# First block of a three-stage kernel: token sums spread over three chunks, seven-product sets from chunk 3 on, squares of chunk 0 on ScalarE

## The chip, the cores and the metric

One NeuronCore of a Trainium2 chip runs the whole program. The metric is the device time in microseconds, the median of several executions.

## The reference

Three stages follow one another. Retention attention (4 batches, 8 heads, 576 positions, 64 per head) gives x of 2304 tokens by 512. A first feed-forward block takes x through 2048 hidden units with a squared ReLU. A second one takes the result through four domains of 1024 hidden units each, weighted by normalised probabilities.

```python
scores = scale * np.matmul(q, k.transpose(0, 1, 3, 2))
attn_out = np.matmul(scores * Dmat[None, :, :, :], v)
x = attn_out.transpose(0, 2, 1, 3).reshape(B * S, H * D)
...
r = np.maximum(x @ w_in, 0.0)
x = (r * r) @ w_out
...
p = domain_probs / (domain_probs.sum(-1, keepdims=True) + 1e-09)
for e in range(4):
    out += p[:, e:e + 1] * (np.maximum(x @ w1[e], 0.0) @ w2[e])
```

The weights of the first block arrive as 64-bit floats.

## The kernel before, in words

Every matrix is split in two fp32r parts, high and low, and a product of two matrices is three products of parts (high by high, high by low, low by high). Tokens lie in five groups: groups 0 to 3 of 512 tokens and group 4 of 256. A chunk is 256 hidden units: chunks 0 to 7 are the first block, later ones the second. For a chunk `layer1` makes two halves (`f`) of 128 hidden units, twelve products each; `square` (line 598) takes ReLU, square, a high copy on ScalarE and a low part on GpSimd (`split`, line 132), with the square on ScalarE or VectorE by its argument `act`. `layer2_1` (line 875) makes four results of six products from them and writes or adds them to `yacc` (lines 888 to 891).

For chunks in `sevens` (line 66) the groups 0 and 1, and 2 and 3, go in pairs through `layer1_seven` (line 675), which makes a two by two block product with seven block products (42 instructions) instead of eight (48). It needs sums of weight blocks (S1 to S4, lines 156 to 173, made with the conversion of the chunk's weights) and sums of token blocks (T1 to T4). The token sums are made once for each pair by the generator `combine` (line 647): four sums on GpSimd, and four times a difference on VectorE (line 663), a high copy on ScalarE (line 668), a low part on VectorE (line 670) and two stores to DRAM (line 673), for each of two halves. As SBUF has no room for both pairs, `load_parts` (line 638) puts reloads from DRAM into the list `pulls`, and `pull` issues one at a time between the products; all of them are DMAs on SyncE's queue, as are the loads of raw weights (`load_piece`, line 80), which wait for a free one of three buffers.

The order of each engine is the order in which the program writes instructions. Background work is a list `work` of generators, and `tick(n)` (line 267) takes n steps from its front. A step is about one VectorE instruction. `from_f64` (line 101) converts one piece of a weight chunk in six steps: five VectorE instructions (lines 114, 116, 118, 120, 125), a magnitude and a high copy on ScalarE, an addition and a subtraction on GpSimd (lines 128 and 129). A chunk has eight pieces, four for each layer. `queue_weights` (line 287) appends the conversion of a chunk two ahead as its buffers come free. `mix` (line 622) weaves `combine` into it, one step of each in turn, the first pair into chunk 1's weights, the second into those of layer 1 of chunk 2. `pace[0]` (line 1182) is the number of steps behind each half of layer 1 and each result of layer 2: 4 in chunks 0 and 1, 2 in chunks 2 to 5. In a set two steps stand behind each block product, ahead of the additions that read it.

The jobs (line 1140) are the layer 1 parts in order; behind each come the layer 2 parts that `behind` names, or all but the latest. Before the first set, in chunk 2, its token sums must be back in SBUF: at job (1, (3,)) the program drains the conversion woven with the second pair's sums, and queues the eight reloads.

Of the kernel before, what the change touches and what calls it, by code (L numbers as in the profile page):

```python
# [26 lines left out]
NW1, NW2 = 8, 16  # L27
# [6 lines left out]
def tile_kernel(ctx, tc, qT, kT, kn, vn, v4d, mask, qdec, kdec, wd, w, probs, probs2, out, outT):  # L34
    nc = tc.nc
# [27 lines left out]
            return slot(t, 2 * g + k // 2)[:, k % 2, :]  # L63
        return t[2][:, GS[4] * k : GS[4] * k + GS[4]]

    sevens = range(2, NW1 - 2)

    def f32(ap):
        return ap.bitcast(F32)
# [195 lines left out]
    work = []  # L265
# [18 lines left out]

    held = {(split_w2, NW1), (split_w1, NW1 + 1)}

    def queue_weights(*place):
        free.update(place)
        while order and order[0] in free and order[0] not in held:
            f, c = order.pop(0)  # L290
            if c >= NW1 + NW2:
                work.extend(stores)
                stores.clear()
                fetch(f, c)
                continue
            splits[f, c] = f(c)
            work.append(splits[f, c])
            work.extend(stores)
            stores.clear()
            if c >= NW1:  # L300
                stores.append(keep(f, c))
# [233 lines left out]
    with tc.manual_schedule():  # L535
# [32 lines left out]
        pace = [2]  # L568
# [6 lines left out]
        def layer1(c, g, between=lambda: None):  # L575
            w1h, w1l = w1s[c]
            wk = lambda t, f, k: t[:, ((A11, A12), (A21, A22))[f][k // 2], k % 2, :]
            hi, lo = hidden(g)
            for f in range(FT):
                h = ps.tile([128, GT], F32, name="h", tag="ps")[:, : GS[g]]  # L580
                n = 0
                for k in range(KT):
                    for a, x in ((w1h, xh_), (w1h, xl_), (w1l, xh_)):
                        nc.tensor.matmul(h, wk(a, f, k), group(x, g, k), start=(n == 0), stop=(n == 3 * KT - 1))  # L584
                        n += 1
                if c < NW1:
                    r = tp.tile([128, GT], F32, name="r")[:, : GS[g]]
                    square(h, r, hi[:, f, :], lo[:, f, :], c in sevens or c == 1)
                else:
                    relu_split(h, hi[:, f, :], lo[:, f, :])  # L590
                tick(pace[0])
                pull()
                if f == 0:
                    extra = between()
            gh[c, g], gl[c, g] = hi, lo
            return extra

        def square(h, r, hi, lo, act=True, stay=False):
            nc.scalar.activation(out=r, in_=h, func=ACTF.Relu)
            if act:  # L600
                nc.scalar.activation(out=r, in_=r, func=ACTF.Square)
            else:
                nc.vector.tensor_tensor(out=r, in0=r, in1=r, op=ALU.mult)
            if stay:
                nc.scalar.copy(out=hi, in_=r)
                nc.vector.tensor_tensor(out=lo, in0=r, in1=f32(hi), op=ALU.subtract)
            else:
                split(r, hi, lo)
# [4 lines left out]
        def pull():  # L613
            if pulls:
                pulls.pop(0)()

        def saved(pair, i, y):
            if (pair, i, y) not in parted:
                parted[pair, i, y] = dram.tile([128, 2 * GT], F32, name=f"parted{pair}_{i}_{y}")
            return parted[pair, i, y].rearrange("p (k n) -> p k n", k=2)  # L620

        def mix(*todo):
            own = [splits[t] for t in todo[:-1]]

            def both():
                for g in own:
                    for _ in g:
                        yield
                        if next(todo[-1], 0) is None:
                            yield  # L630
                yield from todo[-1]

            m = both()
            j = min(j for j, x in enumerate(work) if any(x is g for g in own))
            work[:] = work[:j] + [m] + [x for x in work[j:] if not any(x is g for g in own)]
            splits.update({t: m for t in todo[:-1]})

        def load_parts(pair, what):

# [35 lines left out]
        def layer1_seven(c, ga, gb):  # L675

            w1h, w1l = w1s[c]
            pair = ga // 2
            s = 4 * pair
            own = lambda i: [slot(xh_, s + i), slot(xl_, s + i)]  # L680
            (ha, la), (hb, lb) = hidden(ga), hidden(gb)
            bank = lambda: ps.tile([128, GT], F32, name="h", tag="ps")
            v = nc.vector

            def product(o, i, x, first=True):
                n = 0
                for k in range(2):
                    for a, y in ((w1h, 0), (w1h, 1), (w1l, 0)):
                        nc.tensor.matmul(
                            o, a[:, i, k, :], x[y][:, k, :], start=(first and n == 0), stop=(n == 5),  # L690
                            skip_group_check=True,
                        )
                        n += 1
                tick(2)

            def add(o, x, y):
                v.tensor_tensor(out=o, in0=x, in1=y, op=ALU.add)

            if (c, pair) == (sevens[-1], 1):
                load_parts(0, [("b12", (slot(xh_, 2), slot(xl_, 2)))])  # L700
                load_parts(1, [("b12", (slot(xh_, 6), slot(xl_, 6)))])
            else:
                load_parts(1 - pair, [(i, bufs[i]) for i in (T2, T3, T1, T4)])
            u = [tp.tile([128, GT], F32, name="r") for _ in range(2)]
            u.append(cvp.tile([128, GT], F32, name="cv_tp"))
            b1 = bank()
            product(b1, A11, own(0))
            nc.scalar.copy(out=u[0], in_=b1)
            b6 = bank()
            product(b6, S2, bufs[T2])  # L710
            add(u[1], b6, u[0])
            b7 = bank()
            product(b7, S3, bufs[T3])
            add(u[2], b7, u[1])
            product(b1, A12, own(1), False)
            square(b1, b1, ha[:, 0, :], la[:, 0, :], stay=True)
            pull()
            b5 = bank()
            product(b5, S1, bufs[T1])
            add(u[2], b5, u[2])  # L720
            square(u[2], u[2], hb[:, 1, :], lb[:, 1, :])
            pull()
            product(b7, A22, bufs[T4], False)
            add(u[0], b7, u[1])
            square(u[0], u[0], ha[:, 1, :], la[:, 1, :])
            pull()
            product(b5, S4, own(3), False)
            add(u[1], b5, u[1])
            square(u[1], u[1], hb[:, 0, :], lb[:, 0, :])
            pull()  # L730
            gh[c, ga], gl[c, ga] = ha, la
            gh[c, gb], gl[c, gb] = hb, lb
# [142 lines left out]
        def layer2_1(c, g):  # L875
            w2h, w2l = w2s[c]
            hi, lo = gh.pop((c, g)), gl.pop((c, g))
            for m in range(KT):
                o = ps.tile([128, GT], F32, name="o", tag="ps")[:, : GS[g]]
                n = 0  # L880
                for f in range(FT):
                    for a, x in ((w2h, hi), (w2h, lo), (w2l, hi)):
                        nc.tensor.matmul(  # L883
                            o, a[:, f, 128 * m : 128 * m + 128], x[:, f, :], start=(n == 0), stop=(n == 3 * FT - 1)
                        )
                        n += 1
                y = yacc[g][:, m, :]
                if c == 0:
                    nc.scalar.copy(out=y, in_=o)  # L889
                else:  # L890
                    nc.vector.tensor_tensor(out=y, in0=o, in1=y, op=ALU.add)  # L891
                tick(pace[0])
                pull()
                if c == NW1 - 1 and g < 2:
                    magnitude(g, m, mags[g][m])
                if c == NW1 - 1 and g == NG - 1:
                    split(y, group(xh_, g, m), group(xl_, g, m))
# [263 lines left out]
        bufs["raw"] = [wp.tile([128, 2 * GT], F32, name=f"raw_{n}", tag=n) for n in ("r2hi", "r2lo")]  # L1161
        wide = lambda: [wp.tile([128, 2 * GT], F32R, name=n).rearrange("p (k n) -> p k n", k=2) for n in ("r2hi", "r2lo")]
        bufs["half"] = wide()
        combos = [combine(0), combine(1)]
        for i in range(2):
            for y, t in enumerate((xh_, xl_)):
                nc.sync.dma_start(out=saved(i, "b12", y), in_=f32(slot(t, 4 * i + 2)))
# [8 lines left out]
        for i, job in enumerate(jobs):  # L1176
# [2 lines left out]
            if c < NW1 + NW2:  # L1179
                drain(splits[split_w1, c])  # L1180

            pace[0] = 4 if c in (0, 1) else 3 if c in (p, q) else 4 if c == z else 3 if c >= NW1 and c not in scaled else 2
            if job == (1, (3,)):
                drain(splits[split_w1, 2])
                bufs.update({T2: (slot(xh_, 2), slot(xl_, 2)), T3: bufs["half"], T1: wide(), T4: (slot(xh_, 6), slot(xl_, 6))})
                load_parts(0, [(t, bufs[t]) for t in (T2, T3, T1, T4)])
            if c in sevens:
                while pulls:
                    pull()
# [37 lines left out]
            if g and gs == (4,):  # L1227
                rescale(g, s)
                if g == 3:
                    work.append(sb[0])  # L1230
            if job == (0, (0,)):
                mix((split_w1, 1), (split_w2, 1), combos[0])
            if job == (0, (4,)):
                mix((split_w1, 2), combos[1])
            pend += [(c, (g_,)) for g_ in gs] if c < NW1 else [job]
            todo = behind.get(job)
            if todo is None:
# [104 lines left out]
```

## Time and profile before

| | us |
|---|---|
| median of three runs | 1269.88 |
| lowest and highest of them | 1269.33, 1270.60 |
| the profiled execution, its own time | 1266.78 |
| its span, first to last instruction | 1265.0 |
| PE busy in the span | 1201.6 (95%) |
| VectorE (DVE) busy | 948.8 (75%) |
| GpSimd (POOL) busy | 704.5 (56%) |
| ScalarE (ACT) busy | 478.8 (38%) |

The profile's times start with the first instruction of one execution. PE is TensorE, PEld its loading of weights, SP the engine SyncE, whose queue issues the DMAs. An instruction's duration runs from its start to its end, with any time that it was held after its start in it. A wait is the idle time of an engine ahead of an instruction and is put down to what ended it. The attention stage ends and the first block starts at about 80 us; the second block starts at about 480 us.

### The profile page before, as it was taken

To read this page: it belongs to the slowest core of one execution; us is meant where nothing else is said; L and a number is where in the kernel's file an instruction comes from. 1 tells how busy PE (TensorE), PEld (TensorE's weight loads), DVE (VectorE), ACT (ScalarE), POOL (GpSimd) and SP (SyncE) were. 2 spreads that over 40 slices of the span, in tenths; PEclk is the share of its full clock that TensorE was granted. 3 is DMA by queue.
4 is the path that set the end of the run, shared out by engine and by line. 5 is a ranking of instruction groups with operands and counts; after the bars stand their busy time and mean duration, and the time that the engine had idled before them with its cause. 6 is when DMAs were issued, how large, how long until landed. Compare 5 with 4: busy or idle time off the path is not lost. (4 is left out here: it accounts for less than half of the span.)

```text
span 1265.0 us, 18570 instructions
## 1 busy us (share of the span) xinstructions
PE 1201.6 (95%) x6422; PEld 997.1 (79%) x6422; DVE 948.8 (75%) x1566; ACT 478.8 (38%) x1122; POOL 704.5 (56%) x713
## 2 busy tenths in 40 slices
PE   7999787998999999999999999999999999999997
PEld 6877575776887888788888888888787888888876
DVE  4789988968668658856786777776677778778768
ACT  4554555545444235453433323333322222222221
POOL 5748665544434334454445533555406777777775
PEclk9999898999999999999999999999999999999999
DMA  9942337547553100156525454454667664654651
GB/s 338 319 145 102 131 138 293 211 167 257 188 210 123 36 9 16 62 185 224 206 80 221 175 191 159 151 217 174 258 231 270 206 215 156 211 196 164 222 166 67
DMA packets 93538, 224.27 MB, mean 177 GB/s; under 512 B 11266, under 2 KB 19970, under 8 KB 93444
## 3 DMA queue, kind: packets, MB, share of 16 engines
q1 hardware_dynamic: 92932, 222.38, 49.7%
q8 instruction: 51, 0.84, 0.3%
q10 hardware_dynamic: 512, 0.70, 0.2%
q14 instruction: 43, 0.35, 0.1%
HBM read 149.88 MB, written 73.16 MB: 176 GB/s over the span
## 5 line engine op out<-in xcount | busy, mean ns | idle before, releaser
L923 DVE SCALAR_TENSOR_TENSOR oacc<-o,pr,oacc 128x512 f32<-128x512 f32 x150 | 110.0, 746 | 30.3 <-PE o L915 29.9
L883 PE MATMUL o<-glo,w2hi 128*128 128x512 f32 (+1 forms) x320 | 120.2, 376 | 12.4 <-POOL glo L134 12.4
L1058 DVE TENSOR_TENSOR sums<-sums,h 128x512 f32<-128x512 f32 x202 | 128.5, 678 | 1.9 <-PE h L1048 1.9
L915 PE MATMUL o<-w2hi,ghi 128*128 128x512 f32 x320 | 124.9, 390 | 0.5 <-ACT w2hi L133 0.4
L915 PE MATMUL o<-w2lo,ghi 128*128 128x512 f32 x320 | 124.7, 390 | 0.6 <-POOL w2lo L134 0.6
L915 PE MATMUL o<-w2hi,glo 128*128 128x512 f32 x320 | 124.7, 390 | 0.0
L134 POOL TENSOR_TENSOR glo<-r,ghi 128x512 fp32r<-128x512 f32 (+1 forms) x64 | 78.6, 1232 | 80.9 <-ACT ghi L133 68.8
L883 PE MATMUL o<-ghi,w2hi 128*128 128x512 f32 (+1 forms) x320 | 119.7, 374 | 1.3 <-ACT y L889 1.2
L883 PE MATMUL o<-ghi,w2lo 128*128 128x512 f32 (+1 forms) x320 | 119.3, 373 | 0.0
L891 DVE TENSOR_TENSOR y<-o,y 128x512 f32<-128x512 f32 (+1 forms) x140 | 87.0, 630 | 26.6 <-PE o L883 26.2
L584 PE MATMUL h<-xh,w1hi 128*128 128x256 f32 (+1 forms) x320 | 104.5, 326 | 2.5 <-ACT y L889 1.6
L134 POOL TENSOR_TENSOR w2lo<-wraw,w2hi 128x256 fp32r<-128x256 f32 x64 | 52.0, 837 | 98.1 <-ACT w2hi L133 98.1
L584 PE MATMUL h<-xl,w1hi 128*128 128x256 f32 (+1 forms) x320 | 104.1, 325 | 0.0
L584 PE MATMUL h<-xh,w1lo 128*128 128x256 f32 (+1 forms) x320 | 104.1, 325 | 0.0
L128 POOL TENSOR_TENSOR cv_m<-cv_m,cv_d 128x256 f32<-128x256 f32 x64 | 50.9, 795 | 86.3 <-DVE cv_d L125 74.9
L966 PE MATMUL h<-xh,w1hi 128*128 128x512 f32 x224 | 88.3, 394 | 3.6 <-ACT r L985 2.6
L753 PE MATMUL h<-xh,w1lo 128*128 128x512 f32 x224 | 88.0, 393 | 2.2 <-POOL w1lo L134 2.2
L753 PE MATMUL h<-xh,w1hi 128*128 128x512 f32 x224 | 88.1, 393 | 2.1 <-ACT r L766 1.1
L753 PE MATMUL h<-xl,w1hi 128*128 128x512 f32 x224 | 87.7, 392 | 0.0
L966 PE MATMUL h<-xh,w1lo 128*128 128x512 f32 x224 | 87.4, 390 | 0.2 <-DMA w1lo<-kept 0.2
L966 PE MATMUL h<-xl,w1hi 128*128 128x512 f32 x224 | 87.2, 389 | 0.0
L134 POOL TENSOR_TENSOR r2lo<-cv_m,r2hi 128x256 fp32r<-128x256 f32 x60 | 47.3, 814 | 64.6 <-ACT r2hi L133 55.2
(207 smaller groups left out, 3212.6 us busy)
## 6 DMA issues: line engine op xcount, KB each, us to landing
wraw<-wd SPq DMA_DIRECT2D x64, 256.0 KB, 2.9
wraw<-w SPq DMA_DIRECT2D x64, 256.0 KB, 3.0
xh<-parted SPq DMA_DIRECT2D x16, 512.0 KB, 5.3
xl<-parted SPq DMA_DIRECT2D x16, 512.0 KB, 6.3
r2hi<-parted SPq DMA_DIRECT2D x16, 512.0 KB, 5.9
r2lo<-parted SPq DMA_DIRECT2D x16, 512.0 KB, 6.1
kept<-w1hi SPq DMA_DIRECT2D x16, 512.0 KB, 5.0
kept<-w1lo SPq DMA_DIRECT2D x16, 512.0 KB, 5.7
```

The lines of the kernel that those rows point to most:

```text
L128: nc.gpsimd.tensor_tensor(out=a, in0=a, in1=p, op=ALU.add)
L134: nc.gpsimd.tensor_tensor(out=lo, in0=src, in1=f32(hi), op=ALU.subtract)
L584: nc.tensor.matmul(h, wk(a, f, k), group(x, g, k), start=(n == 0), stop=(n == 3 * KT - 1))
L753: nc.tensor.matmul(o, a[:, i, k, :], slot(x, j)[:, k, :], start=(first and n == 0), stop=(n == 5), skip_group_check=True,)
L883: nc.tensor.matmul(o, a[:, f, 128 * m : 128 * m + 128], x[:, f, :], start=(n == 0), stop=(n == 3 * FT - 1))
L891: nc.vector.tensor_tensor(out=y, in0=o, in1=y, op=ALU.add)
L915: nc.tensor.matmul(o, a[:, f, 128 * m : 128 * m + 128], x[:, f, :], start=(n == 0), stop=(n == 3 * FT - 1))
L923: nc.vector.scalar_tensor_tensor(out=acc, in0=o, scalar=pr[:, tt, e : e + 1], in1=acc, op0=ALU.mult, op1=ALU.add)
L966: nc.tensor.matmul(o, a[:, i, k, :], slot(x, j)[:, k, :], start=(first and n == 0), stop=(n == 5), skip_group_check=True,)
L1058: v.tensor_tensor(out=e, in0=e, in1=b, op=op)
```

## The change

Chunk 2 leaves the sets: `sevens` starts at 3. The two `combine` generators become one, and `woven` takes a step of it behind three of every four conversion steps, in the weights of chunks 1 to 3. Chunk 0 squares on ScalarE too. Behind a half of layer 1 of chunks 0 to 5 come five steps, three for the narrow group, and `pace[0]` is 2 behind the results of layer 2 there. In a set one step stands behind each sum and each square instead of two behind each block product. The writes of chunk 0 into `yacc` move from ScalarE to VectorE. The reloads for the first set are put in line at job (2, (2,)), those of T4 at (2, (3,)) behind its layer 1.

```diff
-    sevens = range(2, NW1 - 2)
+    sevens = range(3, NW1 - 2)
...
+    combos, turns = [], [0]
+
+    def both(x, y):
+        yield from x
+        yield from y
+
+    def woven(gen):
+        for _ in gen:
+            yield
+            turns[0] += 1
+            if combos and turns[0] % 4 and next(combos[0], 0) is None:
+                yield
...
-            splits[f, c] = f(c)
+            splits[f, c] = woven(f(c)) if 0 < c <= sevens[0] else f(c)
...
-                    square(h, r, hi[:, f, :], lo[:, f, :], c in sevens or c == 1)
+                    square(h, r, hi[:, f, :], lo[:, f, :], c < NW1 - 2)
...
-                tick(pace[0])
+                tick((5 if g < 4 else 3) if c < NW1 - 2 else pace[0])
...
-                tick(2)
...
             nc.scalar.copy(out=u[0], in_=b1)
+            tick()
             b6 = bank()
             product(b6, S2, bufs[T2])
             add(u[1], b6, u[0])
+            tick()
             b7 = bank()
             product(b7, S3, bufs[T3])
             add(u[2], b7, u[1])
+            tick()
             product(b1, A12, own(1), False)
             square(b1, b1, ha[:, 0, :], la[:, 0, :], stay=True)
+            tick()
             pull()
             b5 = bank()
             product(b5, S1, bufs[T1])
             add(u[2], b5, u[2])
             square(u[2], u[2], hb[:, 1, :], lb[:, 1, :])
+            tick()
             pull()
             product(b7, A22, bufs[T4], False)
             add(u[0], b7, u[1])
             square(u[0], u[0], ha[:, 1, :], la[:, 1, :])
+            tick()
             pull()
             product(b5, S4, own(3), False)
             add(u[1], b5, u[1])
             square(u[1], u[1], hb[:, 0, :], lb[:, 0, :])
+            tick()
...
-                    nc.scalar.copy(out=y, in_=o)
+                    nc.vector.tensor_copy(out=y, in_=o)
...
-        combos = [combine(0), combine(1)]
+        combos.append(both(combine(0), combine(1)))
...
-            pace[0] = 4 if c in (0, 1) else 3 if c in (p, q) else 4 if c == z else 3 if c >= NW1 and c not in scaled else 2
-            if job == (1, (3,)):
-                drain(splits[split_w1, 2])
+            pace[0] = 3 if c in (p, q) else 4 if c == z else 3 if c >= NW1 and c not in scaled else 2
+            if job == (sevens[0] - 1, (2,)):
+                for _ in combos[0]:
+                    pass
...
-                load_parts(0, [(t, bufs[t]) for t in (T2, T3, T1, T4)])
+                load_parts(0, [(t, bufs[t]) for t in (T2, T3, T1)])
...
-            if job == (0, (0,)):
-                mix((split_w1, 1), (split_w2, 1), combos[0])
-            if job == (0, (4,)):
-                mix((split_w1, 2), combos[1])
+            if job == (sevens[0] - 1, (3,)):
+                load_parts(0, [(T4, bufs[T4])])
```

The function `mix` goes; `combine` and `from_f64` stay as they are.

## Rows read from the trace of the kernel before

**Rows 1.** The page: the span, and PE's busy tenths in 40 slices

```profile
span 1265.0 us, 18570 instructions
...
PE   7999787998999999999999999999999999999997
```

**Rows 2.** Windows: us; busy of PE, PEld, DVE, ACT, POOL (instructions); clock, DMA, GB/s

```profile
79.90:189.80 109.90, 96.66 (x432) 78.16 (x433) 99.77 (x140) 54.02 (x114) 76.46 (x69) 0.95 0.38 132
189.80:249.80 60.00, 49.91 (x231) 39.44 (x230) 52.29 (x98) 31.17 (x69) 34.97 (x40) 0.91 0.71 262
249.80:401.80 152.00, 142.00 (x686) 117.90 (x685) 112.75 (x225) 73.55 (x152) 70.25 (x80) 1.00 0.54 194
401.80:479.10 77.30, 76.86 (x354) 63.71 (x352) 50.88 (x87) 24.77 (x47) 28.79 (x28) 1.00 0.08 26
```

**Rows 3.** Timeline of PE: the second product of layer 1 and one 95 behind

```profile
80.23 0.40 PE L584 MATMUL h<-xl,w1hi 128*128 128x512 f32 x1
...
101.78 0.39 PE L883 MATMUL o<-ghi,w2hi 128*128 128x512 f32 x1
```

**Rows 4.** Waits of PE, 79.9 to 189.8 us: total us, times, longest

```profile
PE o L883 <- POOL glo L134: 10.2, 5, 3.6
```

**Rows 5.** Waits of PE, 189.8 to 249.8 us

```profile
PE h L689 <- DMA xl<-parted: 5.4, 2, 4.6
```

**Rows 6.** Waits of PE, 249.8 to 401.8 us

```profile
PE h L689 <- DVE cv_tp L697: 10.0, 6, 2.7
```

**Rows 7.** DVE's conversion groups, 79.9 to 189.8 us: busy us, mean ns, idle before

```profile
L118 DVE SCALAR_TENSOR_TENSOR cv_m<-wraw,cv_m 128x256 int32<-128x256 int32 x16 | 13.9, 870 | 0.5
...
L116 DVE TENSOR_SCALAR cv_m<-cv_m 128x256 int32<-128x256 int32 x16 | 12.0, 748 | 0.2
...
L125 DVE SCALAR_TENSOR_TENSOR cv_d<-wraw,cv_d 128x256 f32<-128x256 uint32 x15 | 10.5, 697 | 0.5
...
L114 DVE TENSOR_SCALAR cv_m<-cv_m 128x256 f32<-128x256 f32 x16 | 9.2, 578 | 0.0
...
L120 DVE TENSOR_SCALAR cv_d<-cv_m 128x256 int32<-128x256 int32 x15 | 8.3, 553 | 0.5
```

**Rows 8.** Window of line 670 alone (low parts of token sums): DVE busy, count

```profile
79.90:189.80 109.90, 15.64 (x16) 0.95 0.38 132
```

**Rows 9.** Window of line 663 alone (differences of token sums)

```profile
79.90:189.80 109.90, 16.24 (x16) 0.95 0.38 132
```

**Rows 10.** Window of line 603 alone (squares on DVE)

```profile
79.90:189.80 109.90, 10.18 (x10) 0.95 0.38 132
```

**Rows 11.** Window of line 891 alone (additions into y)

```profile
79.90:189.80 109.90, 5.44 (x8) 0.95 0.38 132
```

**Rows 12.** Timeline of DVE: start us, us

```profile
142.16 0.43 DVE L125 SCALAR_TENSOR_TENSOR cv_d<-wraw,cv_d 128x256 f32<-128x256 uint32 x1
142.50 0.29 DVE L114 TENSOR_SCALAR cv_m<-cv_m 128x256 f32<-128x256 f32 x1
...
145.92 1.38 DVE L125 SCALAR_TENSOR_TENSOR cv_d<-wraw,cv_d 128x256 f32<-128x256 uint32 x1
```

**Rows 13.** Timeline of POOL beside it

```profile
144.25 2.77 POOL L657 TENSOR_TENSOR raw_r2hi<-xh,xl 128x512 f32<-128x512 f32 x2
```

**Rows 14.** Waits of SP's DMA queue, 140 to 215 us

```profile
SPq L87 <- DVE cv_d L125: 41.8, 10, 10.0
```

**Rows 15.** The page, DMA issues: KB each, median us to landing

```profile
r2hi<-parted SPq DMA_DIRECT2D x16, 512.0 KB, 5.9
```

**Rows 16.** Timeline of DVE in chunk 4's second set

```profile
337.81 0.69 DVE L606 TENSOR_TENSOR glo<-h,ghi 128x512 fp32r<-128x512 f32 x1 [1.20 <-ACT ghi L605]
338.42 0.28 DVE L120 TENSOR_SCALAR cv_d<-cv_m 128x256 int32<-128x256 int32 x1
...
339.08 0.68 DVE L697 TENSOR_TENSOR cv_tp<-h,cv_tp 128x512 f32<-128x512 f32 x1
```

**Rows 17.** Timeline of PE there: the last product's first instruction

```profile
339.82 0.50 PE L689 MATMUL h<-xh,w1hi 128*128 128x512 f32 x1 [1.17 <-DVE cv_tp L697]
```

More of the change, by code (lines that the diff above doesn't have):

```diff
@@ L620, in saved @@
             return parted[pair, i, y].rearrange("p (k n) -> p k n", k=2)
[L622 to L636, printed above, removed]
         def load_parts(pair, what):
```

## The prediction

> **What bounds the kernel now.** First the page: the tenths of PE are full nearly everywhere but in the slices from about 110 to 210 us [rows 1]. Then the busy times by stage [rows 2]. From 79.9 us, where the first product of layer 1 starts, to 189.8 us, where the first set of seven starts, PE is busy 96.7 of 109.9 us while DVE is busy 99.8: here VectorE is the engine without a pause. From 401.8 us on PE is busy 76.9 of 77.3 us, and nothing can be won.
>
> Busy time hides loss, so I count products. Two products of 512 columns, 95 apart, start at 80.23 and 101.78 us [rows 3]: 0.2268 us each. Up to 401.8 us PE does 216 such units for each of chunks 0 and 1 and 204 for each of chunks 2 to 5 (two sets of 42, 12 for the narrow group, 108 for layer 2), less 48 of chunk 5's layer 2 that come later: 1200 units, 272 us. The stretch lasts 321.9 us, so 50 us are lost. Up to the first set it is 396 units, 89.8 us, in 109.9: 20 us. The other 30 lie in the sets and beside them. What ended the waits: up to 189.8 us the low halves that POOL makes for layer 2 [rows 4]; in the first set reloads of saved token sums [rows 5]; later DVE's add, line 697, which must read a bank before the last product of a set writes it [rows 6]. The granted clock, 0.95 and 0.91 in the first two stages and 1.00 behind them [rows 2], fell behind such waits, so part of the 50 us is half-speed products (1.2 GHz); it is in the 50 already.
>
> **The change, part by part.**
>
> *Chunk 2 leaves the sets.* Two sets of 42 products become 96 plain ones: 12 more, 12 x 0.2268 = **2.7 us** on PE, for certain. With them go ten adds, and the four sums of weights of that chunk, from DVE. The first set now comes after 612 units (three chunks of layer 1, 324; layer 2 of 13 groups, 288): 138.7 us of PE at best, so at 218.6 us.
>
> *Steps and sums before the first set.* Layer 1 now takes 5 steps behind each wide half and 3 behind a narrow one, layer 2 takes 2 behind each product: 3 x 46 + 104 = 242 steps up to the first set. The sums of tokens are 80 of them (two pairs, two halves, 20 each), the sums of chunk 3's weights 7; about 155 are left, 26 conversions of six steps. With the six conversions made during attention these are all 32 pieces of chunks 0 to 3, four more than the first set needs. Three sum steps go with four conversion steps, so 80 need 107 conversion steps; chunks 1 and 2 have 96, and the sums end early in chunk 3's weights, in chunk 2's layer 2 of group 0. The forced finish then finds nothing left. Each step moves all that it issues: the sums' 32 stores on SP's queue and 16 additions on POOL's, spread thinner too. A store waits there for the low part of line 670, and weight loads wait behind it; with three raw buffers ahead that costs nothing as long as DVE is the slower one, and a late weight load would hold ScalarE's magnitude and then DVE if it isn't.
>
> *DVE's bill.* A conversion is five instructions, 870 + 748 + 697 + 578 + 553 ns = 3.45 us [rows 7], with POOL busy 76.5 of 109.9 us. The sums cost 15.6 + 16.2 = 31.9 us [rows 8, 9]. The squares on DVE, 10.2 us [rows 10], go. The additions into y are 0.68 each [rows 11]. As a check on before: 53.9 + 31.9 + 10.2 + 5.4 = 101.4 us against 99.8 busy, a factor 0.984 (durations overlap slightly). After: 26 x 3.45 = 89.6; sums 31.9; 44 wide and 8 narrow writes of y, the narrow ones taken as half, 48 x 0.68 = 32.6; together 154 x 0.984 = **152 us** against PE's 138.7.
>
> The copies of chunk 0's y on DVE are not in the trace as such. The nearest row is the addition two lines below, 0.68 us [rows 11], which reads PSUM as well; bounds 0.4 to 0.8 each, 20 of them (18 wide ones' worth): -5 to +2 us on the bill. ScalarE gives 20 copies and takes ten squares, with 54.0 of 109.9 us busy [rows 2]: nothing; if ScalarE were full, the high halves would be late.
>
> Why 3.45 us: an instruction that meets no POOL work takes 0.43 or 0.29 us; the same one beside POOL's sums of tokens took 1.38 [rows 12, 13]. So the price depends on how often POOL works. POOL had 69 instructions in 109.9 us, 1.11 us each; after it has 102 up to the first set (30 low halves of squares, 52 of conversions, 16 sums, 4 of weights), 113 us of about 147, 0.77 busy against 0.70. I keep 3.45; bounds are 1.73 (three of 0.29, two of 0.43, no meeting) and some 5.2 (twice the waits).
>
> PE may run ahead of DVE. In before, 18 conversions and 12 additions stand ahead of the first set in the program, and 15.6 and 8 were done when it started [rows 7, 11]: about 11 us of DVE work were still open. So a surplus of 13 us costs not 13 but 5 to 11 before the first set: I take **8**, bounds 0 and 20. The set itself then finds some backlog in front of its adds: **3** more.
>
> *Reloads for the first set.* They stood behind weight loads in SP's queue, which waited for DVE 41.8 us in ten waits, up to 10.0 [rows 14]. Now T2, T3 and T1 are put in line one job earlier and land before their products: T2 has 23 us of PE time, T3 and T1 15. T4's pair is issued in the layer 2 behind (2,(3,)), about 12 us before its product; landing takes 5.9 us [rows 15]. A single long wait of SP could make it 4 us late; that lies within the 3 above (bounds 0 and 5).
>
> *Steps behind the sums.* A set of chunk 4 shows the chain [rows 16, 17]: the low half of line 606 waits for ScalarE until 337.81; two conversion steps follow, at 338.42 and behind; the add runs at 339.08, and the last product starts at 339.82 after a wait of 1.17 us. Behind the change one step stands between, 0.33 us less: 0.85, and more where that step meets POOL or the first product behind the pause is slow. I take 1.1. The steps ahead of line 606 were in the shadow of ScalarE anyway. Six sets x 1.1 = **6.6 us** where the six of chunks 3 to 5 waited 10.0 [rows 6]. Bounds 4 and 10. Seven steps a set instead of 14 leave work to the stages around; DVE has 112.8 of 152 us busy there [rows 2], so it is hidden, and without that room each step would cost its 0.3 to 0.6 us.
>
> *Narrow groups.* Layer 2 of the narrow group of the first set's chunk follows its layer 1 by only 2.7 us of other work, so POOL's low half can be late; the longest such wait was 3.6 us [rows 4]: bounds 0 and 3.6, I take **2**.
>
> *Sum.* Lost after: 8 + 3 + 6.6 + 2 = 19.6; before 49.9; products +2.7. Gain 27.6 us. The profiled execution took 1266.8 us around a span of 1265.0, so 1239.2; the three runs' median, 1269.9, lies 3.1 above it, so **1242**.
>
> **Rivals.**
>
> A. *PE is the bound up to the first set.* Sums spread thinner meet less, the price of a conversion falls to 3.0 and the bill to about 140 us. For: before, the same sums were crowded into fewer jobs. Against: POOL's share rises. Then 8 and 3 become 1 and 0, and the time is 1232.
>
> B. *Slower: the meetings of DVE and POOL grow.* Place: from about 120 us to the first set. It decides if that start comes later than 254 us (8 becomes 36 lost, the gain gone). If no instruction of the two engines overlapped at all, it is 26 x 1.73 + 32 x 0.68 = 67 us of DVE (each at its free price) plus 113 of POOL: 180 us, the set at 260, lost 41, and the time 1242 + 33 = 1275. Against: the same sum over before gives 15.6 x 1.73 + 21.8 + 6.1 + 76.5 = 131 us where 109.9 passed, so they do overlap partly; scaled by that, 180 is 151, the bill above. The Trainium skill, SBUF — State Buffer, section Who interferes with whom, says that such a pair shares an exclusive lock, whoever comes first blocking the other wholly. By that rule the time is rival B's; the 1.38 us row agrees with it in kind, the 131 against 109.9 doesn't in full.
>
> C. *The backlog lives on.* DVE comes to the sets late, so the adds wait as before (10 instead of 6.6), T4 is late in the first set (3 becomes 10), and the start loses 11. Time 1242 + 3 + 3.4 + 7 = 1255. For: layer 2's steps cost DVE about 6 us per 5.4 us of PE. Against: the half layers have room.
>
> That the sums are not spread as said is excluded by the count of steps above.
>
> **How the numbers follow.** My forecast 0.55, A 0.27, C 0.12, B 0.05, about 0.01 between C and B. The range 1230 to 1255 takes in A, the forecast with its bounds and about half of C; it leaves out B and what of C goes further. A measurement of this kernel tells 0.2%, 2.5 us, from no change: faster 0.93, same 0.02, slower 0.05.
>
> **What would show it.** Right: the first set starts at 225 to 232 us; no wait of over 2 us on reloads; up to there DVE is busy over 95%; waits of about 1 us before each set's last product; no loss behind chunk 5. A: the set starts below 222 us. B: above 250, with conversions above 4.5 us each. Wrong altogether: a stall after 400 us of before's work that was not there, or DVE with pauses while PE waits, which would point at ScalarE or SP.

## The result, and the profile after

The changed kernel takes **1241.28 us** (median of four runs, 1240.72 to 1241.79), the kernel before 1269.99 (four runs): ratio 0.9774, 95% interval 0.9757 to 0.9791, so 28.7 us faster. The forecast was 1242 within 1230 to 1255. The profiled execution took 1241.8 us around a span of 1240.0. The profiled execution of before was 3.2 us below this median of its kernel and that of after 0.5 us above its own, so the two profiles are only 25.0 us apart.

The page of the kernel after, its span and PE's tenths, to lay beside [rows 1]:

```profile
span 1240.0 us, 18533 instructions
...
PE   7999999799999999999999999999999999999997
```

Its stages, cut at the same places of the program as [rows 2] (columns: stage, its length, busy time and instructions of PE, PEld, DVE, ACT, POOL, granted clock, DMA share, GB/s):

```profile
80.20:221.70 141.50, 140.62 (x672) 117.88 (x673) 135.10 (x207) 73.93 (x150) 99.78 (x93) 1.00 0.39 134
221.70:254.80 33.10, 26.43 (x140) 22.17 (x139) 27.43 (x52) 18.91 (x43) 20.70 (x24) 0.90 0.64 232
254.80:374.90 120.10, 115.78 (x548) 95.51 (x547) 101.84 (x193) 60.24 (x125) 59.86 (x68) 1.00 0.57 202
374.90:452.20 77.30, 76.86 (x353) 63.72 (x351) 53.35 (x92) 25.26 (x49) 31.25 (x31) 1.00 0.09 31
452.20:1240.00 787.80, 771.14 (x3574) 639.70 (x3574) 580.94 (x910) 252.32 (x555) 448.03 (x439) 0.99 0.50 178
```

Apart from the first and the last slice, the one hole that is left in PE's tenths lies in the second of these stages. In [rows 1] the slices at eight tenths or less reach from 126 to 221 us (the prediction says about 110 to 210), and one more stands at 285 us. Up to the first set PE is now busy 140.6 of 141.5 us at a clock of 1.00, where it was 96.7 of 109.9 at 0.95. Counted as in the prediction, 1212 units of 0.2267 us (274.8) stand against the 294.7 us from the first product of layer 1 to chunk 6, so **19.9 us are lost**, where 49.9 were. The last stage takes 1.9 us longer than its counterpart of before did, 787.8 against 785.9 us:

```profile
479.10:1265.00 785.90, 769.02 (x3574) 638.55 (x3574) 581.28 (x910) 252.54 (x555) 448.30 (x439) 1.00 0.50 178
```

The program is the same there and PE's busy time differs by about as much (769.0 and 771.1); I did not follow this further.

What ended PE's waits after (us in total, times, longest), in the first three of those stages in turn:

```profile
...
PE o L886 <- POOL w2lo L129: 0.8, 2, 0.6
...
PE h L686 <- ACT r L704: 4.9, 1, 4.9
PE h L686 <- DVE y L894: 1.6, 1, 1.6
...
PE h L686 <- DVE cv_tp L693: 3.6, 6, 0.8
PE h L686 <- ACT r L704: 0.7, 1, 0.7
```

POOL's 10.2 us of [rows 4] are gone, so are the reloads of [rows 5], and the waits in the sets fell from 10.0 in six sets [rows 6] to 3.6 in the five behind the first. New are two waits in the first set: 1.6 us for a bank that DVE's addition into y (line 894) must empty, and 4.9 us on ScalarE. The timelines of DVE, ACT and PE (start us, us) show the links of the longer one:

```profile
230.97 0.83 DVE L118 SCALAR_TENSOR_TENSOR cv_m<-wraw,cv_m 128x256 int32<-128x256 int32 x1
...
231.83 0.40 ACT L127 CAST w2hi<-cv_m 128x256 fp32r<-128x256 f32 x1 [0.88 <-DVE cv_m L118]
232.15 0.58 ACT L704 COPY r<-h 128x512 f32<-128x512 f32 x1
...
221.72 0.40 PE L686 MATMUL h<-xh,w1hi 128*128 128x512 f32 x1
...
232.78 0.79 PE L686 MATMUL h<-xh,w1hi 128*128 128x512 f32 x1 [4.89 <-ACT r L704]
...
240.76 0.39 PE L886 MATMUL o<-ghi,w2hi 128*128 128x512 f32 x1
```

ScalarE takes its instructions in order. The copy of the set's first product (line 704) needs nothing but that product, which PE finished about 9 us earlier, but it stands behind a cast of weights that waits for DVE, and DVE is that far behind. PE must not write the bank again before it is copied. From 221.72 to 240.76 us are 19.04 us for 42 products, 9.52 us of work: 9.5 us lost in this set, a part of it products at half speed behind the wait (0.43 us apart instead of 0.23 up to 236.4 us, clock 0.90 in the stage).

DVE's groups in the stage up to the first set, to lay beside [rows 7] (count, busy us, mean ns):

```profile
L118 DVE SCALAR_TENSOR_TENSOR cv_m<-wraw,cv_m 128x256 int32<-128x256 int32 x23 | 19.3, 838 | 0.3
L116 DVE TENSOR_SCALAR cv_m<-cv_m 128x256 int32<-128x256 int32 x23 | 17.4, 758 | 0.5
...
L125 DVE SCALAR_TENSOR_TENSOR cv_d<-wraw,cv_d 128x256 f32<-128x256 uint32 x23 | 15.5, 673 | 0.4
L114 DVE TENSOR_SCALAR cv_m<-cv_m 128x256 f32<-128x256 f32 x23 | 15.0, 653 | 1.4 <-ACT cv_m L98 1.4
L120 DVE TENSOR_SCALAR cv_d<-cv_m 128x256 int32<-128x256 int32 x23 | 14.1, 615 | 1.1
L892 DVE COPY y<-o 128x512 f32<-128x512 f32 x16 | 10.9, 680 | 0.0
```

A conversion costs 838 + 758 + 673 + 653 + 615 ns = 3.54 us (forecast 3.45), a copy of y 0.680 (0.68). Of 26 conversions 23 are done when the set starts.

The chain in a set, as in [rows 16, 17], here the last set of chunk 5:

```profile
360.82 0.69 DVE L619 TENSOR_TENSOR glo<-h,ghi 128x512 fp32r<-128x512 f32 x1 [2.31 <-ACT ghi L618]
361.43 0.41 DVE L125 SCALAR_TENSOR_TENSOR cv_d<-wraw,cv_d 128x256 f32<-128x256 uint32 x1
361.76 0.69 DVE L693 TENSOR_TENSOR cv_tp<-h,cv_tp 128x512 f32<-128x512 f32 x1
...
362.50 0.50 PE L686 MATMUL h<-xh,w1hi 128*128 128x512 f32 x1 [0.84 <-DVE cv_tp L693]
```

One step stands between where two stood, and the last product waits 0.84 us instead of 1.17.

### The profile page after: what moved, and what is told of

Read it like the earlier page. It is cut to its first block, busy times and chain, and to the rows that moved or that the text cites. A ratio compares the mean times of both kernels' runs of the same rounds, so it can differ in the third digit from the quotient of the medians.

```text
span 1240.0 us, 18533 instructions
## 1 busy us (share of the span) xinstructions
PE 1199.5 (97%) x6434; PEld 999.5 (81%) x6434; DVE 951.9 (77%) x1560; ACT 473.3 (38%) x1106; POOL 705.6 (57%) x711
## 4 chain that ended last, share of the span: by engine, by line
PE 70%; DVE 17%; issue 4%; ACT 4%; POOL 3%; DMA 2%; ACTq 0%; SPq 0%; DVEq 0%; POOLq 0%
PE o L918 15%; PE h L756 11%; PE h L969 10%; PE h L1051 10%; PE o L886 9%; PE h L597 8%; PE h L686 3%; DVE y L894 2%; DVE cv_m L118 2%; PE qk L400 1%; DVE xl L845 1%; DVE cv_d L125 1%; DVE cv_m L116 1%; PE xo L452 1%; DVE cv_d L120 1%
## 5 line engine op out<-in xcount | busy, mean ns | idle before, releaser
L134 POOL TENSOR_TENSOR glo<-r,ghi 128x512 fp32r<-128x512 f32 (+1 forms) x68 | 86.2, 1272 | 69.9 <-ACT ghi L133 59.1
L597 PE MATMUL h<-xh,w1hi 128*128 128x256 f32 (+1 forms) x352 | 116.8, 332 | 0.8 <-DVE xl L487 0.8
L597 PE MATMUL h<-xl,w1hi 128*128 128x256 f32 (+1 forms) x352 | 116.8, 332 | 0.0
L597 PE MATMUL h<-xh,w1lo 128*128 128x256 f32 (+1 forms) x352 | 116.7, 332 | 0.0
```

What stands on the lines that cost most here:

```text
L134: nc.gpsimd.tensor_tensor(out=lo, in0=src, in1=f32(hi), op=ALU.subtract)
```

## The experiments

All are the changed kernel with one edit (the last two with those of earlier experiments too), each with its ratio to the kernel before on the same chip. 0.001 is 1.27 us; the changed kernel is at 0.9774.

**Chunk 0's copies back on ScalarE.**

```diff
-                    nc.vector.tensor_copy(out=y, in_=o)
+                    nc.scalar.copy(out=y, in_=o)
```

> The changed kernel with one part undone: chunk 0's results go back to ScalarE. Theory (DVE's bill up to the first set is the last limit; PE runs ahead of it and pays in the first set, 9.5 us lost there): 16 x 0.68 + 4 x 0.41 = 12.6 us leave DVE, the loss in the first set falls to about 1 to 3 us, time 1233 to 1236. Rival (ScalarE's chain becomes late, as where PE waited for ScalarE's copies before): waits of PE on ScalarE's copies come back and the time is 1241 to 1246.

1236.26 us, ratio 0.9722 (0.9706 to 0.9738), about 6.6 us better than the changed kernel. The gain (5.0 us by the medians) is near what was expected, its place is not: the first set still loses 7.1 us, and 12.5 us of copies fewer leave DVE hardly emptier. The same stretch of time in the changed kernel and in this one, whose first product comes 1.4 us later, at 81.59 us, and whose set starts at 221.32:

```profile
80.20:221.30 141.10, 140.22 (x669) 117.48 (x670) 134.70 (x207) 73.55 (x149) 99.55 (x93) 1.00 0.38 134
```

```profile
80.20:221.30 141.10, 140.29 (x687) 118.54 (x683) 132.33 (x194) 84.61 (x174) 103.41 (x97) 1.00 0.41 142
```

Cut at each program's own first product and set, DVE is busy 131.6 of 139.7 us instead of 135.1 of 141.5, so 3.5 us less. One conversion more is in it, and a conversion's price rose to 3.65 us (811 + 778 + 731 + 655 + 678 ns). The token sums rose from 31.0 to 32.6 us. So of the 12.5 us about a third came back as longer instructions in SBUF, a third went into one more conversion, and the rest left DVE emptier. That the longer instructions are waits for POOL, beside which the copies had run, fits the experiment without POOL's sums below, but was not tested by itself. ScalarE's extra 11 us (84.6 of 141.1) hurt nobody: the rival is excluded.

**Chunk 0's squares back on VectorE.**

```diff
-                    square(h, r, hi[:, f, :], lo[:, f, :], c < NW1 - 2)
+                    square(h, r, hi[:, f, :], lo[:, f, :], 0 < c < NW1 - 2)
```

> The changed kernel with one part undone: the squares of chunk 0 go back to VectorE. Theory (DVE's bill): some 10 us more on DVE, no room for it, so 7 to 10 us longer: 1248 to 1251, lost before and in the first set. Rival (PE's lead hides it, or ScalarE was the limit): 1240 to 1243.

1247.75 us, ratio 0.9811 (0.9795 to 0.9828): 4.7 us worse (6.5 by the medians), between the two expectations. The work is paid at once, in chunk 0's own layer 2, where PE waits for DVE to empty a bank, and goes on at half speed for some products behind:

```profile
PE o L886 <- DVE y L892: 3.2, 1, 3.2
```

The first set loses 9.5 us as in the changed kernel, though DVE is busy 8 us longer before it (143.3 and 135.1 us). This does not show that the work before the set is of no matter to it: PE has lost 9.0 us by then instead of 2.8, so most of the 8 us is paid already, and DVE stands as far behind PE at the set as in the changed kernel (10.4 us, by the table in the next section).

**Steps ahead of the sums in the sets, as before.**

```diff
                         n += 1
+                tick(2)
...
-            tick()
```

> The changed kernel with one part undone: in the sets two steps behind each block product, ahead of the sums, as before. Theory: the waits of the last product of the six sets go back from 3.6 to about 10 us in chunks 3 to 5: 1246 to 1248. Rival (position is of no matter, the waits were backlog): waits under 5 us, 1240 to 1243.

(All seven `tick()` of the set go.) 1248.77 us, ratio 0.9824 (0.9810 to 0.9839): 6.3 us worse. The sets of chunks 3 to 5 from the second on wait

```profile
PE h L686 <- DVE cv_tp L694: 7.2, 6, 2.7
```

instead of 3.6 us, with 1.17 again in the steady sets and 2.7 where the steps are sums of weights. Less than the 10 us expected, but the waits come back with the steps. The edit changes two things, the place of the steps and their number in a set (14 for 7), and the run does not tell which of them matters; the other 2.7 us lie in slow products behind the longest wait and in layer 2 of the narrow groups.

**Sets from chunk 2 on.**

```diff
-    sevens = range(3, NW1 - 2)
+    sevens = range(2, NW1 - 2)
```

> The changed kernel with one part undone: sets from chunk 2 on, so the token sums have only the weights of chunks 1 and 2 to stand between and the first set comes 49 us of PE earlier. Theory (the sums need a third plain chunk to hide in): the 2.7 us of products come back, but DVE has about 100 us of work against 90 of PE and the forced finish of the last sums, so 8 to 20 us more are lost at the first set: 1244 to 1258. Rival (pace, squares and order did it, not the third chunk): 1238 to 1241.

1257.03 us, ratio 0.9887 (0.9872 to 0.9902): 14.4 us worse, as the theory said. PE waits here:

```profile
PE o L886 <- ACT ghi L133: 12.9, 1, 12.9
```

The sums are not finished when the reloads must be queued, so the rest is forced out in one piece ahead of layer 2's operands. A stretch of DVE's timeline shows what such a piece costs:

```profile
171.91 0.68 DVE L660 TENSOR_TENSOR raw_r2hi<-raw_r2lo,raw_r2hi 128x512 f32<-128x512 f32 x1
173.32 0.69 DVE L667 TENSOR_TENSOR r2lo<-raw_r2hi,r2hi 128x512 fp32r<-128x512 f32 x1 [0.73 <-ACT r2hi L665]
173.93 0.68 DVE L660 TENSOR_TENSOR raw_r2lo<-raw_r2lo,raw_r2hi 128x512 f32<-128x512 f32 x1
```

Each sum waits for ScalarE's high copy of itself, 2.0 us a sum instead of 1.3, and the squares that layer 2 needs stand behind it all in ScalarE's queue. Two plain chunks are too few for the sums at this number of steps.

**No sums of high and low token parts on POOL.** The token sums are taken of the high parts alone; POOL's 16 additions are left out, and DVE's instructions stay.

```diff
-                    nc.gpsimd.tensor_tensor(
-                        out=r[i - s], in0=f32(slot(xh_, i)[:, k, :]), in1=f32(slot(xl_, i)[:, k, :]), op=ALU.add
-                    )
-                b11, b21, b12, b22 = (r[i] for i in range(4))
-                for i, o, x, y in ((T1, b11, b12, b11), (T3, b12, b22, b12), (T2, b11, b22, b11), (T4, b21, b21, b11)):
+                b11, b21, b12, _ = (r[i] for i in range(4))
+                x11, x21, x12, x22 = (f32(slot(xh_, s + i)[:, k, :]) for i in range(4))
+                for i, o, x, y in ((T1, b11, x12, x11), (T3, b12, x22, x12), (T2, b11, x22, b11), (T4, b21, x21, b11)):
```

> The changed kernel without POOL's 16 sums of high and low token parts (the token sums take the high parts alone); DVE's instructions, their order and the steps stay as they are. Theory (DVE instructions that read and write SBUF wait for POOL's to end): POOL loses 23 of its 100 us up to the first set, so DVE's price of a conversion falls from 3.54 to about 3.0 us and the differences of token sums from 1.17 to under 1 us; the loss in the first set falls from 9.5 to 1 to 4, time 1233 to 1237. Rival (the waits have nothing to do with POOL's load): 3.5 us a conversion, 1240 to 1242.

1234.82 us, ratio 0.9708 (0.9670 to 0.9746). DVE's groups up to the first set:

```profile
L118 DVE SCALAR_TENSOR_TENSOR cv_m<-wraw,cv_m 128x256 int32<-128x256 int32 x24 | 16.3, 678 | 0.4
L116 DVE TENSOR_SCALAR cv_m<-cv_m 128x256 int32<-128x256 int32 x24 | 15.2, 634 | 0.6
L125 DVE SCALAR_TENSOR_TENSOR cv_d<-wraw,cv_d 128x256 f32<-128x256 uint32 x24 | 14.0, 583 | 0.4
L114 DVE TENSOR_SCALAR cv_m<-cv_m 128x256 f32<-128x256 f32 x25 | 14.0, 558 | 1.7 <-ACT cv_m L98 1.7
L120 DVE TENSOR_SCALAR cv_d<-cv_m 128x256 int32<-128x256 int32 x24 | 13.0, 541 | 1.4
```

A conversion costs 2.99 us where it cost 3.54, by the same instructions: 0.55 us of each were waits for POOL's additions. The Trainium skill, SBUF — State Buffer, section Who interferes with whom, names the lock behind it; the fall to 2.99 agrees. The differences of token sums fell from 1.17 to 1.00 us, where under 1 was expected. The time agrees too, but again not the place: the first set still loses 6.5 us, with two thirds of its wait left:

```profile
PE h L684 <- ACT r L702: 3.3, 1, 3.3
```

**Sums behind every step of a conversion.**

```diff
-            if combos and turns[0] % 4 and next(combos[0], 0) is None:
+            if combos and next(combos[0], 0) is None:
```

> The changed kernel with the token sums behind every conversion step instead of three of four, so that they end 27 conversion steps earlier and the conversions come later; the work up to the first set is the same. Theory (the total of DVE's work up to the first set counts, not how thin the sums lie): within 3 us of the changed kernel, 1239 to 1244. Rival (what won was the thinner spread): waits for POOL's low halves in chunk 1 as before, 1246 or more.

1247.87 us, ratio 0.9808 (0.9780 to 0.9836): about 4.3 us worse, for the rival's side, though not for its reason. The wait is not for layer 2's low halves but for its weights:

```profile
PE o L886 <- POOL w2lo L129: 7.6, 4, 4.1
```

With the same number of steps, more sums mean that the conversion of chunk 1's second weights comes later, and layer 2 of chunk 1 meets it: 10.0 us are lost there, while the first set loses 5.6 instead of 9.5. Three in four seems to be about as many sums as the deadline of the weights allows (no ratio between was run); the changed kernel's 0.8 us of waits are the same wait.

**Fewer steps just before the first set.** Two experiments had changed the total of DVE's work before the set by 8 to 12 us and left the set's loss near 7 to 9.5, so I formed another theory: the backlog is made in the last 20 us, where the sums are over, every step is a conversion's, and four conversions run that nobody needs yet.

```diff
-                tick((5 if g < 4 else 3) if c < NW1 - 2 else pace[0])
+                tick((1 if g > 3 else 2) if c == sevens[0] - 1 and g > 2 else (5 if g < 4 else 3) if c < NW1 - 2 else pace[0])
...
+            if job in ((sevens[0] - 1, (3,)), (sevens[0] - 1, (4,))):
+                pace[0] = 1
```

> The changed kernel with fewer steps just before the first set: 2 and 1 instead of 5 and 3 behind the halves of chunk 2's groups 3 and 4, and 1 instead of 2 behind the results of layer 2 between; 14 steps (over two conversions, whose weights nobody needs yet) move behind the set. Theory (what the first set loses is a backlog of DVE made in the last 20 us, where every step is a conversion's, and not the total up to there): the loss in the first set falls from 9.5 to about 2 us, the half-speed products there go, 1233 to 1235, ratio about 0.972. Rival (the backlog is the sum of all work since 80 us, or the work moved comes back in the set): 1239 to 1242.

1235.50 us, ratio 0.9715 (0.9698 to 0.9733). The first set now loses 2.0 us, and this is all that PE waits for in it:

```profile
PE h L686 <- DVE cv_tp L693: 0.8, 1, 0.8
PE h L686 <- ACT r L704: 0.5, 1, 0.5
```

Part of it comes back: the second set loses 3.9 instead of 2.2 us, as the 14 steps stand before it now. The time is what the theory said; that the backlog is made in the last 20 us is not what the trace of the changed kernel shows (the table in the next section).

**Both: fewer steps, and the copies on ScalarE.** The edits of the first experiment and of the one just above together.

> Fewer steps before the first set, and chunk 0's results on ScalarE too. Theory: the two gains lie in different places and add: the small waits up to the set (2.6 us) go with the copies, the first set's with the steps: 1230 to 1233, ratio about 0.970. Rival (both paid for the same backlog): as the better of the two alone, 1233 to 1236.

**1232.25 us**, ratio 0.9688 (0.9670 to 0.9706), 9 us below the changed kernel by the medians and 11 by the ratios, the fastest of all with the next one. The gains add for the greater part: 1.0 us is lost up to the set where it was 2.8, 1.2 us in it, 5.2 in the second. The sets of chunks 3 to 5 together wait

```profile
PE h L686 <- DVE cv_tp L693: 4.2, 6, 0.8
PE h L686 <- ACT r L704: 2.8, 1, 2.8
```

**Fewer steps behind the narrow groups too.**

```diff
-            if job in ((sevens[0] - 1, (3,)), (sevens[0] - 1, (4,))):
+            if job in ((sevens[0] - 1, (3,)), (sevens[0] - 1, (4,)), (sevens[0], (4,))):
```

> The version before it (fewer steps before the first set, copies on ScalarE) with 1 step instead of 2 behind the eight narrow results of layer 2 between the first and the second set, where each product takes 0.68 us of PE and two steps take DVE longer. Theory (the second set's wait of 2.8 us on ScalarE's first copy, with half-speed products behind, is the same local backlog, now made by the steps moved behind the set): the second set loses about 1 to 2 us instead of 5.2, time 1228 to 1230, ratio about 0.966. Rival (the steps only move on, to the next set or to a forced finish of the weights ahead of chunk 4): 1232 or more.

1232.25 us, ratio 0.9695 (0.9670 to 0.9720): no gain. The second set's loss falls from 5.2 to 1.5 us as expected, and the fourth's rises from 1.3 to 2.7, where ScalarE's first copy is late once more:

```profile
PE h L686 <- DVE cv_tp L693: 5.0, 6, 1.2
PE h L686 <- ACT r L704: 1.3, 1, 1.3
```

The profile loses 2.2 us less in the first block than the version before, but begins that block 2.3 us later (82.7 against 80.4 us), behind an attention stage that no edit touches, and takes 2.3 us longer behind it, where no edit reaches either; between profiles that start was anywhere from 78.8 to 82.7. What this edit wins is no more than one execution differs from the next.

## Why the prediction was right, and where it was not

*The size.* Forecast 19.6 us lost, measured 19.9; 2.7 us of products more; 1242 against 1241.3. That it fits so closely is partly luck, since the loss lies elsewhere than I put it.

*The place of the loss* is the step that failed: "I take 8" before the first set and 3 in it, and the start between 225 and 232 us. Measured: 2.8 lost before it, start at 221.7 (the sign given for rival A), and 9.5 in the set, where 3 of backlog and 1.1 for the chain were forecast (the chain's own wait there was 0.2 us). I had shown that PE may run some 11 us ahead of DVE and did not draw the conclusion that a surplus of 13 is then met almost whole at the first place where PE needs DVE or ScalarE soon, which is the set. I also named only the adds as waiting there; the longest wait was ScalarE's copy behind a cast of weights.

The traces bear this out. In the changed kernel the last product of the last layer 2 result ahead of the set and DVE's addition that empties its bank start at

```profile
218.62 0.39 PE L886 MATMUL o<-ghi,w2lo 128*128 128x512 f32 x1
...
229.03 0.68 DVE L894 TENSOR_TENSOR y<-o,y 128x512 f32<-128x512 f32 x1
```

so DVE stands 10.4 us behind PE when the set begins. The same two starts in the other traces, with what the first set loses:

| kernel | DVE behind PE, us | lost in the first set, us |
|---|---|---|
| changed kernel | 10.4 | 9.5 |
| squares on VectorE | 10.4 | 9.5 |
| steps ahead of the sums | 10.4 | 9.8 |
| copies on ScalarE | 8.0 | 7.1 |
| no sums on POOL | 6.9 | 6.5 |
| sums behind every step | 6.4 | 5.6 |
| fewer steps before the set | 5.6 | 2.0 |
| fewer steps, copies on ScalarE | 3.2 | 1.2 |

The set takes back nearly all of the lag, and less where fewer steps stand between that addition and the set. The lag is not made in the last 20 us: in the changed kernel it is 8.0 us at the first result of layer 2, 8.6 at 177 us and 10.3 at 192. Where the lag is smaller before, it does grow late: without POOL's sums it is 0.9 us at 175 us and 6.9 at 217.

*The total of 152 us* for DVE's bill holds in its prices (conversion 3.54 for 3.45, sums of tokens 31.0 for 31.9, copies 0.68 for 0.68), but not as a bound. Taking 12.5 us of copies off DVE took 2.4 us off the set's loss, adding 9.8 us of squares left it as it was, and moving two conversions (some 8 us) from just before the set to behind it took 7.5 us off. What counts for the set is how far DVE is behind PE when it comes: work early on is partly paid before, in waits of PE or in pauses of DVE, and work just ahead of the set almost in full.

*The squares and the copies.* The squares' move is worth 4.7 us by the ratios, 6.5 by the medians (I had 10 on DVE's bill). The copies' move was taken as part of the bill; it costs 6.6 us by the ratios, 5.0 by the medians, so this part of the change makes it slower.

*Chunk 2 out of the sets:* the third plain chunk is worth 14 us, its 2.7 us of products already counted. *The steps behind the sums:* 6.3 us, of which one step less in front of the last sum, 0.33 us a set, is the small part (0.84 for 1.17 in a steady set, forecast 0.85); the set whose steps are sums of weights alone gives 3.3 us (4.3 lost there for 1.0). *The reloads* never made PE wait, as said. *The narrow groups* lost 0.3 us, not 2.

*The rivals.* A had the start of the set right, but its price of a conversion (3.0 us, measured 3.54) and its time, 1232, wrong: the set paid. B, no overlap of DVE and POOL at all, is excluded: it put the start at 260 us. That POOL's work sets the price of DVE's is shown by the experiment without POOL's sums. C was right in that the backlog reaches the first set, wrong in that it stays: the five later sets wait about 4 us, where 10 were put for six.

*Left open:* the 1.9 us in the second block, which lie within what two executions of an unchanged stretch differed by here (2.3 us in the last two experiments). The parts undone one by one (14.4, 6.3, 4.7 and 4.3 us for the spread of the sums, less 6.6 for the copies) come to 23 of the 28.7 us by the ratios; the new number of steps before the first set and the earlier reloads were not undone alone, so how the rest divides is not shown. Whether the sums could be spread over two chunks with more steps was not tried.

## What to carry to other kernels

Background work that has a deadline should be spread so that each few microseconds of the leading engine carry no more of it than the helper can do in them, and least of all just ahead of a short dependency, where the leader gives back its head start; a total that fits is not enough (without POOL's sums DVE was busy 125 of 140 us and the set still lost 6.5). Look at what stands in the queue in front of the instruction that such a dependency needs: here a cast of weights, needed by nobody soon, held up a copy that TensorE waited for. Do not price work on a helper by its busy time: 12.5 us of copies taken off VectorE won 5.0 us by the medians, and 9.8 us of squares put back on it cost 6.5. Here that was two fifths of the one and two thirds of the other.

## What the runs showed of the hardware

VectorE's instructions that read PSUM took the same time with GpSimd busy 70% of the stretch and 57% without its sums (copies 0.68 us, additions 0.68 us in both), while the same conversion instructions, in SBUF alone, cost 3.54 us in the one and 2.99 in the other, with 23 us of GpSimd's sums more or less beside them. I had counted both kinds into one bill. The two engines' times do not simply add, though: rival B's count of no overlap gives 180 us for a stretch that took 141.5.
